# Block-sparse attention and a gated feed-forward on one core: attention output turned by DMA transposes, attention packed into the first half of the output stage, loads tied to the gate/value stages

## The chip, the core and the metric

The kernel runs on one core of a Trainium2 chip. The core has five engines with their own instruction queues: TensorE (PE, matmuls and weight loads), VectorE (DVE), ScalarE (ACT), GpSimd (POOL) and SyncE (SP, which here only issues DMAs). Each executes its queue in order; they wait for each other through semaphores. DMAs issued by SyncE and by GpSimd share the core's 16 DMA engines. The metric is the device time of one execution in microseconds, the median of several runs; smaller is better.

## The reference

Inputs q, k and v have 4 batches, 8 heads, 768 positions and 64 features. Each query attends to keys less than 16 positions away and, beside them, to 24 block summaries (one per 32 keys). The result, as a matrix x of 3072 tokens by 512 features, goes through a gated feed-forward layer with a gated residual.

```python
k_sum = k.reshape(B, H, nb, block, D).max(axis=3)     # block 32, nb 24
v_sum = v.reshape(B, H, nb, block, D).mean(axis=3)
scores_l = scale * q @ k^T, masked to |i - j| < 16
scores_s = scale * q @ k_sum^T + log(32)
a = softmax(concat(scores_l, scores_s))
x = a @ concat(v, v_sum)                              # -> [3072, 512]
g = x @ w_gate;  val = x @ w_val                      # 512 -> 1536
ffn_out = (gelu(g) * val) @ w_out                     # 1536 -> 512
out = x + sigmoid(x @ w_res) * ffn_out
```

## The kernel before

**Units and stages.** The tokens are worked in 8 units (u = 0 to 7) of 384 tokens, two for each batch b: half = 0 and half = 1. The loop over units is at the end of the kernel. For each unit there is a gate/value stage and an output stage. The gate/value stage runs 12 steps over fo (fo_step): four matmuls for g and four for vv (one for each quarter ko of the 512 features of x, L307), Gelu on ScalarE (L312), and the product gvT on VectorE (L313). g and vv live in PSUM tiles with the tag mm, of which there are four (ps_mm). The output stage of unit u (mid_out for u = 1 to 6, first_out for 0, last_out for 7) works, for each of three groups (sub) of 128 tokens, a residual gate (res_step: r, then tanh), 12 matmuls over gvT and w_out (ffn_step: f, L339), and a closing step on VectorE (end_step: th, o) that ends in an output DMA on SyncE.

**Attention inside the output stage.** While unit u's output stage runs, the attention of unit u+1 is worked between its matmuls. For each of four head pairs hp: s_step (12 small matmuls of kW against qT, L267, into the one PSUM buffer of ps_s; exp on ScalarE to P, L271; mask on VectorE, L274), and later av_step (12 small matmuls of P against vext, L285; reciprocal L289 and product L291 on VectorE give xn). Then xt_step turns the 128 features of a pair with three TensorE transposes (xp, L296), and VectorE copies them (L298) to xT, whose quarters ko the next gate/value stage reads as the moving operand. s_step, av_step and xt_step are written into mid_out by hand, and their place in the code is their place in each engine's queue.

**Keys, queries and values of the next batch.** For batch 0 and 1, k and q are turned on TensorE (k_step, q_step). For batches 2 and 3 they are loaded by GpSimd DMAs, cast to bf16, into k_nat (12 DMAs) and q_nat (6 DMAs) (load_nat), followed by 12 v loads into vext (v_loads). turn_all then issues two DMA transposes on SyncE: k_nat to kW (L124) and q_nat to qT (L126). It stands after step fo = 6 of the gate/value stage of units 2 and 4; the loads are first in the code of those units, and nothing but free buffers holds GpSimd back from issuing them. In the gate/value stages of units 3 and 5, v_rims copies the neighbouring rows of v by DMAs on SyncE, vsum_grp computes block means of v (12 matmuls, a VectorE cast to vpart, four small SyncE DMAs to vsum), vsum_bc spreads them with four GpSimd copies (L257), and k_blocks, after steps fo = 4 to 7, computes the block maxima of k for one head pair (L199 reduce, L203 copy, both VectorE). k_rims (GpSimd, L207 and L208) copies neighbouring key columns after the transpose of k.

The lines that the steps of the prediction touch:

```python
xn = st["xn"].rearrange("p s (h d) -> p s h d", d=D)[:, :, 2 * hp:2 * hp + 2, :]   # [128, NSUB, DM]
nc.tensor.transpose(xp[:, sub * 128:(sub + 1) * 128],
                    st["xn"][:, sub, ko * 128:(ko + 1) * 128], ident[:])
copy(st["xT"][:, ko, :], xp[:])
```

Of the kernel before, what the change touches and what calls it, by code (L numbers as in the profile page):

```python
# [9 lines left out]
BF16 = mybir.dt.bfloat16  # L10
# [5 lines left out]
def kernel(  # L16
# [11 lines left out]
    nc = tc.nc  # L28
# [41 lines left out]
    bgrp = const.tile([QT, 3, 32], BF16, name="bgrp")  # L70
    warm = const.tile([128, 512], BF16, name="warm")
    gate1 = const.tile([1, 1], F32, name="gate1")
    kW = [const.tile([128, NT, NP, 128], BF16, name=f"kW{i}") for i in range(2)]
    qT = [const.tile([128, NQ, NP, 128], BF16, name=f"qT{i}") for i in range(2)]
    k_nat = const.tile([QT, NT, DM], BF16, name="k_nat")
# [9 lines left out]
    def load_qk(src, b, parts, name):  # L85
        t = qk.tile([PP, H, PJ, D], BF16, tag=name, name=name)
        hs = H // parts
        for i in range(parts):
            nc.gpsimd.dma_start(
                out=t[:, i * hs:(i + 1) * hs].rearrange("p h j d -> p h (j d)"),  # L90
                in_=src[b, i * hs:(i + 1) * hs].rearrange("h (p j) d -> p h (j d)", j=PJ),
            )
        return t
# [18 lines left out]

    k_sb, q_sb = {}, {}

    def load_nat(b):
        for t in range(NT):
            nc.gpsimd.dma_start(out=k_nat[:, t].rearrange("p (h d) -> p h d", d=D),  # L117
                                in_=k[b, :, t * QT:(t + 1) * QT, :].rearrange("h p d -> p h d"))
        for c in range(NQ):
            nc.gpsimd.dma_start(out=q_nat[:, c].rearrange("p (h d) -> p h d", d=D),  # L120
                                in_=q[b, :, c * 128:(c + 1) * 128, :].rearrange("h p d -> p h d"))

    def turn_all(b):
        nc.sync.dma_start_transpose(out=kW[b % 2].rearrange("d t g k -> d (t g) k")[:, :, 0:QT],  # L124
                                    in_=k_nat.rearrange("p t f -> p (t f)"))
        nc.sync.dma_start_transpose(out=qT[b % 2].rearrange("d c g k -> d (c g) k"),  # L126
                                    in_=q_nat.rearrange("p c f -> p (c f)"))

    with tc.manual_schedule():
# [147 lines left out]
        def av_step(u, hp, st, pool=ps_o, tag="ao"):  # L277
            b, half = u // 2, u % 2
            P = st["P", hp]
            ao = pool.tile([128, NSUB, 2, D + 1], F32, tag=tag, name="ao")  # L280
            for sub in range(NSUB):
                for hh in range(2):
                    for e in range(2):
                        t = 2 * sub + e
                        nc.tensor.matmul(ao[64 * e:64 * e + 64, sub, hh, :], P[:, hh, t, :],  # L285
                                         vext[b % 2][:, half * HT + t, 2 * hp + hh, 0:D + 1],
                                         start=True, stop=True, skip_group_check=True)
            rz = work.tile([128, NSUB, 2, 1], F32, tag="rz", name="rz")
            nc.vector.reciprocal(rz[:], ao[:, :, :, D:D + 1])  # L289
            xn = st["xn"].rearrange("p s (h d) -> p s h d", d=D)[:, :, 2 * hp:2 * hp + 2, :]  # L290
            nc.vector.tensor_mul(xn, ao[:, :, :, 0:D], rz.to_broadcast([128, NSUB, 2, D]))  # L291

        def xt_step(u, ko, st, pool, tag, copy=nc.vector.tensor_copy):
            xp = pool.tile([128, TU], BF16, tag=tag, name="xp")
            for sub in range(NSUB):
                nc.tensor.transpose(xp[:, sub * 128:(sub + 1) * 128],  # L296
                                    st["xn"][:, sub, ko * 128:(ko + 1) * 128], ident[:])
            copy(st["xT"][:, ko, :], xp[:])  # L298

        def new_unit():  # L300
            return {"xn": upool.tile([128, NSUB, DM], BF16, tag="xn", name="xn"),
                    "xT": upool.tile([128, KO, TU], BF16, tag="xT", name="xT")}


# [13 lines left out]
        def fo_step(st, gvT, fo):  # L318
# [3 lines left out]
            gv_mm(vv, w_val, st, fo, range(KO))  # L322
            gv_end(gvT, fo, g, vv)

        def res_step(st, sub):
            ss = slice(sub * 128, (sub + 1) * 128)
            r = mm_tile("r")
            for ko in range(KO):
                nc.tensor.matmul(r[:], st["xT"][:, ko, ss], w_res[:, ko, :],  # L329
                                 start=(ko == 0), stop=(ko == KO - 1))  # L330
            st["th", sub] = work.tile([128, DM], F32, tag="th", name="th")
            nc.scalar.activation(st["th", sub][:], r[:], AF.Tanh, scale=0.5)  # L332

        def ffn_step(st, gvT, sub, lo, hi):
            ss = slice(sub * 128, (sub + 1) * 128)
            if lo == 0:
                st["f", sub] = mm_tile("f")
            for fo in range(lo, hi):
                nc.tensor.matmul(st["f", sub][:], gvT[:, fo, ss], w_out[:, fo, :],  # L339
                                 start=(fo == 0), stop=(fo == FO - 1), skip_group_check=True)  # L340

        def end_part(u, st, sub, f, cs):
            th = st["th", sub]
            n = cs.stop - cs.start
            nc.vector.scalar_tensor_tensor(th[:, cs], th[:, cs], 1.0, f[:, 0:n], ALU.add, ALU.mult)  # L345
            o = work.tile([128, n], F32, tag="o", name="o")
            nc.vector.scalar_tensor_tensor(o[:], th[:, cs], 0.5, st["xn"][:, sub, cs], ALU.mult, ALU.add)  # L347
            row = u * TU + sub * 128
            nc.sync.dma_start(out=out[row:row + 128, cs], in_=o[:])

# [121 lines left out]

        def mid_out(u, st, gvT, nst):
            n = u + 1
            s_step(n, 0, nst)
            res_step(st, 0)
            ffn_step(st, gvT, 0, 0, FO)
            av_step(n, 0, nst)
            s_step(n, 1, nst)
            end_step(u, st, 0)  # L480
            res_step(st, 1)
            ffn_step(st, gvT, 1, 0, 4)
            av_step(n, 1, nst)
            s_step(n, 2, nst)
            ffn_step(st, gvT, 1, 4, FO)
            av_step(n, 2, nst)
            s_step(n, 3, nst)
            xt_step(n, 0, nst, ps_t, "t")
            end_step(u, st, 1)
            res_step(st, 2)  # L490
            ffn_step(st, gvT, 2, 0, 4)
            av_step(n, 3, nst)
            xt_step(n, 1, nst, ps_t, "t")
            ffn_step(st, gvT, 2, 4, FO)
            xt_step(n, 2, nst, ps_t, "t")
            xt_step(n, 3, nst, ps_mm, "mm")
            end_step(u, st, 2)

        def last_out(u, st, gvT):
# [4 lines left out]
                end_step(u, st, sub)  # L504
            last_step(u, st, gvT, NSUB - 1)

        for u in range(NU):
            b, half = u // 2, u % 2
            nb = b + 1
            if half == 0 and nb < B:  # L510
                if nb == 1:
                    k_sb[nb] = load_qk(k, nb, 1, "k_sb")
                    v_loads(nb)
                    for i in range(2):
                        q_sb[2 * nb + i] = load_q(nb, i)
                else:
                    load_nat(nb)
                    v_loads(nb)
            if u:
                gvT = upool.tile([128, FO, TU], BF16, tag="gvT", name="gvT")  # L520
            for fo in range(0 if u else 2, FO):
                fo_step(st, gvT, fo)
                if u == 0 and fo >= 8:
                    q_step(0, 1, fo - 8, ps_t, "t")
                if u == 2 and fo < NP:
                    q_step(1, 1, fo, ps_t, "t")
                if half == 0 and 1 < nb < B and fo == 6:
                    turn_all(nb)
                    k_rims(nb, slice(0, NP), nc.gpsimd)
                if half == 1 and nb < B:  # L530
                    if fo == 0:
                        v_rims(nb, 0, NT)
                    if fo == (4 if nb == 1 else 0):
                        vsum_grp(nb, ps_t, "t")
                        for i in range(4):
                            vsum_bc(nb, 3 * i, 3 * i + 3, nc.gpsimd)
                    if nb == 1:
                        if fo < NP:
                            k_step(nb, fo, ps_t, "t")
                        elif 7 <= fo < 7 + NP:  # L540
                            q_step(nb, 0, fo - 7, ps_t, "t")
                    elif 4 <= fo < 4 + NP:
                        k_blocks(nb, fo - 4)
            if u == NU - 1:
                last_out(u, st, gvT)
            else:
                nst = new_unit()
                (mid_out if u else first_out)(u, st, gvT, nst)
                st = nst
# [30 lines left out]
```

The softmax here doesn't subtract the row's maximum and nothing guards it: scores larger than these inputs give would overflow.

## Time and profile before

| what | value |
|---|---|
| median of 4 runs | 277.73 us (277.55 to 277.99) |
| the profiled execution | 278.43 us, of which the span of the instructions is 276.7 us |
| granted TensorE clock, mean | 0.997 |
| busy: TensorE, VectorE, ScalarE, GpSimd | 265.1, 162.0, 128.5, 101.0 us |
| transposes of x on TensorE (xp) | 96, of which 72 in the six stages of mid_out |
| q0 (GpSimd's DMAs) | 14.69 MB |
| q1 (SyncE's DMAs) | 10.96 MB |

The profile is of one execution. Spans, starts and durations are microseconds from the span's start unless marked ns. A group of instructions is named by its line, engine and the tiles it writes and reads. The chain that ended last is followed back from the last instruction, at each step to what released it. Matmuls are pipelined, and the chain counts them from end to end, so that its lengths add up. A DMA's row on SPq or POOL is the time that the issuing engine spent on it; its landing comes later.

### The profile page before, as it was taken

Reading aid. Unit: us, or ns where it says so; the run is one execution under the profiler, and the core shown is the slowest. Engines: PE = TensorE matmul, PEld = TensorE weight load, DVE = VectorE, ACT = ScalarE, POOL = GpSimd, SP = SyncE. Lnnn points to the kernel's source line nnn. Section 1 sums busy time; section 2 is a strip of 40 time slices with the busy share of each in tenths; the row PEclk is TensorE's granted clock in tenths of the full one; section 3 lists DMA queues with packets and bytes.
Section 4 is the critical chain, followed back from the end, with each engine's and each line's share of the span. In section 5 each row is a group of like instructions: output and inputs, shape, how many; then the busy total and the mean of one; then the engine's idle time right before and its main releaser. Section 6 shows DMA issues by size and latency. Waiting matters only on the chain.

```text
span 276.7 us, 5879 instructions
## 1 busy us (share of the span) xinstructions
PE 265.1 (96%) x2377; PEld 142.8 (52%) x2377; DVE 162.0 (59%) x365; ACT 128.5 (46%) x204; POOL 101.0 (36%) x134
## 2 busy tenths in 40 slices
PE   7889989999999999999899999999899999999994
PEld 2445644555545555446444565446444565555543
DVE  5856423598338533685947743685947743684424
ACT  1776347375565446343255336343256336343320
POOL 8795572340699942000799832000800000000000
PEclk9999999999999999999999999999999999999998
DMA  6999999999089999114099998104001100111003
GB/s 89 167 130 200 196 204 206 157 157 168 5 53 140 188 154 153 39 39 94 2 69 130 194 168 130 40 38 94 2 0 40 76 2 0 40 39 40 0 0 114
DMA packets 91274, 26.00 MB, mean 94 GB/s; under 512 B 75176, under 2 KB 88304, under 8 KB 91248
## 3 DMA queue, kind: packets, MB, share of 16 engines
q0 software_dynamic: 63664, 14.69, 57.4%
q1 hardware_dynamic: 27584, 10.96, 19.0%
q8 instruction: 18, 0.29, 0.4%
q14 instruction: 8, 0.07, 0.1%
HBM read 29.36 MB, written 6.29 MB: 129 GB/s over the span
## 4 chain that ended last, share of the span: by engine, by line
PE 76%; DMA 11%; DVE 5%; POOL 4%; issue 2%; ACT 1%; POOLq 0%; DVEq 0%
PE f L339 21%; PE g L307 19%; PE vv L307 18%; PE r L329 7%; DMA w_out<-in_moe_w_out_dram 5%; DMA w_gate<-in_moe_w_gate_dram 4%; PE ao L285 3%; PE s L267 3%; DMA q_sb<-in_q_dram 3%; PE xp L296 2%; DVE ks L199 2%; DVE gvT L313 2%; POOL vext L104 1%; PE f L360 1%; PE tp L224 1%
## 5 line engine op out<-in xcount | busy, mean ns | idle before, releaser
L313 DVE TENSOR_TENSOR gvT<-ge,vv 128x384 bf16<-128x384 f32 x96 | 52.6, 552 | 58.7 <-PE vv L307 56.6
L312 ACT ACTIVATE ge<-g 128x384 f32<-128x384 f32 x96 | 47.0, 490 | 82.8 <-DVE gvT L313 42.9
L307 PE MATMUL g<-xT,w_gate 128*128 128x384 bf16 x384 | 80.1, 326 | 1.8 <-DVE gvT L313 1.4
L307 PE MATMUL vv<-xT,w_val 128*128 128x384 bf16 x384 | 78.4, 326 | 1.0 <-DVE gvT L313 1.0
L339 PE MATMUL f<-w_out,gvT 128*128 128x512 bf16 x276 | 65.5, 379 | 0.1
L307 PEld LDWEIGHTS <-w_val 128*128 128x128 bf16 x384 | 37.4, 98 | 27.1 <-issue 2.7
L307 PEld LDWEIGHTS <-w_gate 128*128 128x128 bf16 x384 | 35.7, 98 | 26.8 <-issue 5.0
L271 ACT ACTIVATE P<-s,bias_t 128x768 bf16<-128x768 f32 x32 | 28.8, 901 | 31.8 <-PE s L267 31.6
L257 POOL COPY vext<-vsum 32x1536 bf16<-32x1536 bf16 x14 | 20.0, 1465 | 62.6 <-DMA vsum<-vpart 62.6
L339 PEld LDWEIGHTS <-gvT 128*128 128x128 bf16 x276 | 26.0, 98 | 29.7 <-DMA w_out<-in_moe_w_out_dram 0.6
L104 POOL DMA_DIRECT2D vext<-in_v_dram x48 | 33.0, 731 | 14.5 <-DMA w_out<-in_moe_w_out_dram 5.6
L274 DVE TENSOR_TENSOR P<-P,maskt 128x768 bf16<-128x768 bf16 x32 | 17.7, 556 | 20.6 <-ACT P L271 18.9
L329 PE MATMUL r<-w_res,xT 128*128 128x512 bf16 x96 | 24.3, 381 | 0.0
L345 DVE SCALAR_TENSOR_TENSOR th<-th,f 128x512 f32<-128x512 f32 (+1 forms) x25 | 16.5, 658 | 6.1 <-PE f L339 5.8
L291 DVE TENSOR_TENSOR xn<-ao,rz 128x384 bf16<-128x384 f32 x32 | 17.8, 557 | 1.1
L347 DVE SCALAR_TENSOR_TENSOR o<-th,xn 128x512 f32<-128x512 f32 (+1 forms) x25 | 16.8, 670 | 0.9
L117 POOL DMA_DIRECT2D k_nat<-in_k_dram x24 | 16.3, 749 | 0.0
L199 DVE TENSOR_REDUCE ks<-kW 128x24 bf16<-128x768 bf16 x16 | 15.1, 943 | 1.6 <-ACT kW L214 1.5
L332 ACT ACTIVATE th<-r 128x512 f32<-128x512 f32 x24 | 14.2, 594 | 3.4 <-PE r L329 2.9
L285 PEld LDWEIGHTS <-P 128*64 128x64 bf16 x384 | 8.7, 110 | 13.6 <-DVE P L274 6.4
L289 DVE RECIPROCAL rz<-ao 128x6 f32<-128x6 f32 x32 | 6.1, 192 | 16.2 <-PE ao L285 16.1
L285 PE MATMUL ao<-vext,P 128*64 128x65 bf16 x384 | 12.2, 199 | 0.7 <-DVE vext L238 0.7
(69 smaller groups left out, 189.4 us busy)
## 6 DMA issues: line engine op xcount, KB each, us to landing
out_dram<-o SPq DMA_DIRECT2D x23, 256.0 KB
vext<-in_v_dram POOLq DMA_DIRECT2D x48, 64.0 KB, 6.2
q_sb<-in_q_dram POOLq DMA_DIRECT2D x4, 384.0 KB, 8.7
w_gate<-in_moe_w_gate_dram POOLq DMA_DIRECT2D x6, 256.0 KB, 9.9
w_val<-in_moe_w_val_dram POOLq DMA_DIRECT2D x6, 256.0 KB, 10.7
w_out<-in_moe_w_out_dram POOLq DMA_DIRECT2D x3, 512.0 KB, 14.1
k_nat<-in_k_dram POOLq DMA_DIRECT2D x24, 64.0 KB, 3.1
q_nat<-in_q_dram POOLq DMA_DIRECT2D x12, 128.0 KB, 5.8
```

Source lines behind the costliest of these rows:

```text
L104: nc.gpsimd.dma_start(out=vext[b % 2][0:QT, t, :, 0:D], in_=v[b, :, t * QT:(t + 1) * QT, :].rearrange("h p d -> p h d"))
L199: nc.vector.tensor_reduce(out=ks.rearrange("d (t n) -> d t n", n=2), in_=kw[:, :, 0:QT].rearrange("d t (n w) -> d t n w", w=BLK), axis=myb ...
L257: eng.tensor_copy(vext[b % 2][96:128, lo:hi, :, 0:D], src)
L271: nc.scalar.activation(P.rearrange("p a t q -> p a (t q)"), s[:, :, 0:TU], AF.Exp, scale=scale, bias=bias_t[:])
L274: nc.vector.tensor_mul(Pf, Pf, maskt.unsqueeze(1).to_broadcast([128, 2 * HT, QT]))
L285: nc.tensor.matmul(ao[64 * e:64 * e + 64, sub, hh, :], P[:, hh, t, :], vext[b % 2][:, half * HT + t, 2 * hp + hh, 0:D + 1], start=True, st ...
L291: nc.vector.tensor_mul(xn, ao[:, :, :, 0:D], rz.to_broadcast([128, NSUB, 2, D]))
L307: nc.tensor.matmul(ps[:, 0:TU], w[:, ko, fo * 128:(fo + 1) * 128], st["xT"][:, ko, :], start=(ko == 0), stop=(ko == KO - 1), skip_group_ch ...
L312: nc.scalar.activation(ge[:], g[:, 0:TU], AF.Gelu)
L313: nc.vector.tensor_mul(gvT[:, fo, :], ge[:], vv[:, 0:TU])
L329: nc.tensor.matmul(r[:], st["xT"][:, ko, ss], w_res[:, ko, :], start=(ko == 0), stop=(ko == KO - 1))
L339: nc.tensor.matmul(st["f", sub][:], gvT[:, fo, ss], w_out[:, fo, :], start=(fo == 0), stop=(fo == FO - 1), skip_group_check=True)
```

## The change

- xn gets the layout [128, KO, NSUB, 128], so that the features of one head pair lie together. The last VectorE operation of end_part reads it in that shape.
- For units 2 to 7 (the attention that mid_out works) xt_step is replaced by xt_dma: one DMA transpose per head pair, issued by SyncE right after that pair's av_step. Unit 1 (first_out) keeps xt_step.
- In mid_out all four s_steps and av_steps stand among the matmuls of the first token group; av_step alternates between the PSUM pools ps_o and ps_t. res_step and ffn_step of groups 1 and 2 follow, and end_step of group 0 comes after the last av_step.
- fo_first (units 2 to 7) works quarters 0 to 2 of both g and vv before quarter 3 of both. fo_last_two (units 1 to 7) works g of the last two steps before vv of both.
- load_nat and turn_all are split. pool_after, a one-element GpSimd copy that reads the product gvT of step 0, stands ahead of the k and v loads (units 2 and 4, after step 0) and of the q loads (units 3 and 5, after step 0). turn_k stays after step 6 of units 2 and 4; turn_q goes to step 1 of units 3 and 5, after vsum_grp and vsum_bc, which move there from step 0.
- v_rims is split: the lower half at step 0 of odd units, the upper half at step 1 of the next even unit. k_blocks goes from steps 4 to 7 to steps 8 to 11; since steps 10 and 11 are worked together at step 10, two of them come after the stage's last product.

```diff
+        def xt_dma(ko, st):
+            nc.sync.dma_start_transpose(out=st["xT"][:, ko].rearrange("d (s k) -> d s k", k=128),
+                                        in_=st["xn"][:, ko].rearrange("p s d -> p (s d)"))
...
-            return {"xn": upool.tile([128, NSUB, DM], BF16, tag="xn", name="xn"),
+            return {"xn": upool.tile([128, KO, NSUB, 128], BF16, tag="xn", name="xn"),
...
+        def fo_first(st, gvT):
+            g, vv = mm_tile("g"), mm_tile("vv")
+            for kos in (range(KO - 1), (KO - 1,)):
+                gv_mm(g, w_gate, st, 0, kos)
+                gv_mm(vv, w_val, st, 0, kos)
+            gv_end(gvT, 0, g, vv)
+
+        def fo_last_two(st, gvT):
+            g = [mm_tile("g"), mm_tile("g")]
+            for i in range(2):
+                gv_mm(g[i], w_gate, st, FO - 2 + i, range(KO))
+            for i in range(2):
+                vv = mm_tile("vv")
+                gv_mm(vv, w_val, st, FO - 2 + i, range(KO))
+                gv_end(gvT, FO - 2 + i, g[i], vv)
...
         def mid_out(u, st, gvT, nst):
             n = u + 1
+            other = dict(pool=ps_t, tag="t")
             s_step(n, 0, nst)
             res_step(st, 0)
-            ffn_step(st, gvT, 0, 0, FO)
+            ffn_step(st, gvT, 0, 0, 2)
+            s_step(n, 1, nst)
+            ffn_step(st, gvT, 0, 2, 5)
             av_step(n, 0, nst)
-            s_step(n, 1, nst)
+            xt_dma(0, nst)
+            ffn_step(st, gvT, 0, 5, 6)
+            s_step(n, 2, nst)
+            ffn_step(st, gvT, 0, 6, 8)
+            av_step(n, 1, nst, **other)
+            xt_dma(1, nst)
+            ffn_step(st, gvT, 0, 8, 9)
+            s_step(n, 3, nst)
+            ffn_step(st, gvT, 0, 9, FO)
+            av_step(n, 2, nst)
+            xt_dma(2, nst)
+            res_step(st, 1)
+            av_step(n, 3, nst, **other)
+            xt_dma(3, nst)
             end_step(u, st, 0)
-            res_step(st, 1)
-            ffn_step(st, gvT, 1, 0, 4)
-            av_step(n, 1, nst)
-            s_step(n, 2, nst)
-            ffn_step(st, gvT, 1, 4, FO)
-            av_step(n, 2, nst)
-            s_step(n, 3, nst)
-            xt_step(n, 0, nst, ps_t, "t")
+            ffn_step(st, gvT, 1, 0, FO)
+            res_step(st, 2)
             end_step(u, st, 1)
-            res_step(st, 2)
-            ffn_step(st, gvT, 2, 0, 4)
-            av_step(n, 3, nst)
-            xt_step(n, 1, nst, ps_t, "t")
-            ffn_step(st, gvT, 2, 4, FO)
-            xt_step(n, 2, nst, ps_t, "t")
-            xt_step(n, 3, nst, ps_mm, "mm")
+            ffn_step(st, gvT, 2, 0, FO)
             end_step(u, st, 2)
...
+        def pool_after(x):
+            nc.gpsimd.tensor_copy(gate2[:], x)
...
+                if half == 0 and 1 < nb < B and fo == 0:
+                    pool_after(gvT[0:1, 0, 0:1])
+                    load_k_nat(nb)
+                    v_loads(nb)
+                if half == 0 and b and fo == 1:
+                    v_rims(b, HT, NT)
                 if half == 0 and 1 < nb < B and fo == 6:
-                    turn_all(nb)
+                    turn_k(nb)
                     k_rims(nb, slice(0, NP), nc.gpsimd)
                 if half == 1 and nb < B:
                     if fo == 0:
-                        v_rims(nb, 0, NT)
-                    if fo == (4 if nb == 1 else 0):
+                        v_rims(nb, 0, HT)
+                        if nb > 1:
+                            pool_after(gvT[0:1, 0, 0:1])
+                            load_q_nat(nb)
+                    if fo == (4 if nb == 1 else 1):
                         vsum_grp(nb, ps_t, "t")
                         for i in range(4):
                             vsum_bc(nb, 3 * i, 3 * i + 3, nc.gpsimd)
+                        if nb > 1:
+                            turn_q(nb)
...
-                    elif 4 <= fo < 4 + NP:
-                        k_blocks(nb, fo - 4)
+                    elif 8 <= fo < 8 + NP:
+                        k_blocks(nb, fo - 8)
```

## The prediction

> **What bounds the kernel now.** I read the page's busy table first, then the chain that ended last, stage by stage.
>
> ```profile
> PE 265.1 (96%) x2377; PEld 142.8 (52%) x2377; DVE 162.0 (59%) x365; ACT 128.5 (46%) x204; POOL 101.0 (36%) x134
> PE 76%; DMA 11%; DVE 5%; POOL 4%; issue 2%; ACT 1%; POOLq 0%; DVEq 0%
> ```
>
> From about 56 us on TensorE is the chain. So time goes if a matmul leaves TensorE's queue or a gap in it closes, and comes if TensorE waits for something new. The chain of one output stage (unit 4) and the start of the next gate/value stage (columns: start, length, what):
>
> ```profile
> 179.38 0.31 PE ao L285 x12
> 179.69 0.28 PE s L267 x12
> 179.97 0.27 PE xp L296 x3
> 180.25 0.86 PE r L329 x4
> ...
> 182.28 0.27 PE xp L296 x3
> 182.56 1.73 PE f L339 x8
> 184.28 0.34 PE xp L296 x6
> 184.62 0.87 PE g L307 x4
> 185.49 0.65 PE vv L307 x4
> ```
>
> The transposes (xp) lie on the path, and the first g group takes 0.87 us where later ones take 0.65, because its last transposed quarter comes late: 0.22 us. The stage takes 13.92 us (170.70 to 184.62). A plain gate/value stage is 15.82 (216.89 to 232.71): 24 groups of 0.65 plus that 0.22. Stages of units 3 and 5 hold the value-sum matmuls too (0.76), so should take 16.58, but take 18.64 (122.31 to 140.95) and 18.35 (184.62 to 202.97). VectorE and GpSimd there (start, length):
>
> ```profile
> 133.04 1.52 DVE L203 COPY kW<-ks 128x288 bf16<-128x288 bf16 x1
> ...
> 138.74 0.23 DVE L203 COPY kW<-ks 128x288 bf16<-128x288 bf16 x1
> ```
>
> ```profile
> 133.01 5.71 POOL L257 COPY vext<-vsum 32x1536 bf16<-32x1536 bf16 x4 [23.99 <-DMA vsum<-vpart]
> ```
>
> The same VectorE copy takes 0.23 us alone and 1.5 beside the GpSimd broadcast. The gvT products queue behind it, PSUM buffers come free late, and TensorE loses 2.06 + 1.77 = 3.8 us. Last, the DMA transposes that exist already, on SyncE's queue, and the q loads ahead of them:
>
> ```profile
> 157.41 5.88 SPq L124 DMA_TRANSPOSE kW<-k_nat  x1
> 163.60 5.36 SPq L126 DMA_TRANSPOSE qT<-q_nat  x1
> ```
>
> ```profile
> 146.68 5.39 POOL L120 DMA_DIRECT2D q_nat<-in_q_dram  x6
> ...
> 168.55 0.77 POOL L207 COPY kW<-kW 128x704 bf16<-128x704 bf16 x1 [7.14 <-DMA kW<-k_nat]
> ```
>
> kW lands at 168.55, 5.3 us after its issue ended, with v loads in flight. The DMA engines fall quiet at about 170.4, so qT lands some 1.4 us after its issue ends (168.96). In the earlier pair the issues took 6.97 and 7.68.
>
> [...] the issues take 7 us beside more load traffic, 5.4 beside less. [...] The trace moved 284 and 290 GB/s at 168 to 170 us, so 5.36 us may be contention rather than the transpose's own cost.
>
> **The change, part by part.** T is the start of a gate/value stage, S of an output stage.
>
> *Transposes off TensorE, six output stages.* By matmul starts the 12 transposes fill 0.18 + 0.18 + 0.33 = 0.69 us. The late 0.22 goes as well, since fo_first uses quarter 3 last, a microsecond into the stage. The new order changes between small attention tiles and full matmuls more often. Such a change costs 0.1 (r 0.97 after s against 0.86, f 1.83 against 1.73); I count eight places (each s before r or f, each av before r or f) against five, so +0.3. Net -0.61, times 6: **-3.7 us**. VectorE's 24 copies (0.35 each) leave too, worth nothing by themselves as VectorE is 8.7 of 14 us busy there.
>
> *The packed attention.* av 0 is queued S+2.7 after s, r, two f, s, three f (0.28+0.97+0.43+0.28+0.75). Its P needs exp and mask: in the trace P was ready 2.75 us after s began, 1.28 of it table load. fo_last_two computes both last g groups 1.3 us before the stage's end, so the last Gelu and the table load lie under vv; P is then ready by about S+2.1. The single s buffer is freed by each exp about 1.0 us after its s; the next s comes 1.3, 1.35 and 1.15 later. That cover is 0.15 to 0.35 us. Price without it: perhaps 0.5 a stage. I take 0.
>
> *The DMA transposes of x.* One is an eighth of qT's, so 5.36/8 = 0.67 us of issue by proportion. xn of pair 0 is ready at S+4.2, of pair 3 at S+8.1; the last is issued by S+8.9 and lands about 2 us later, S+11. It is needed at S+13.5 plus a microsecond. I take 0; a fixed cost per transpose that the two large ones can't show is bounded below by 0. Up to about 2.3 us each the four still fit (4.2+4x2.3+1.5 = 14.9); beyond that TensorE waits in all six stages. Behind them on SyncE are only the output stores, for which nobody waits with three o buffers.
>
> *k and v loads gated, units 2 and 4.* The gate opens at T+2.2 (gv product of fo 0). Twelve k loads (8.2 to 9 us) end at T+11.3, land 3.1 later; turn_k waits on SyncE until T+14.3 and issues to T+20.2. Queued behind it: the x transposes, whose first input is ready at S+4.2 = T+20.0. kW lands by T+25.5, twelve v loads (0.7 each, to T+19.7) competing; the x quarters follow by about T+27. They are needed at T+29.2. Hidden, 2 us to spare; beyond that it costs one for one, twice. The gate keeps k loads out of the output stage but not the last v loads, which run some 4 us into it. v_rims, k_rims and the next vsum read these data a stage later.
>
> *q gated, units 3 and 5: a new wait on the path.* Gate at T+2.2; six q loads end issue at T+7.6. In the trace q loads landed 1.3 us apart (4.2 us after the first issue, 6.5 after the last, 4.3 later). First landing about T+5.5, last T+12 beside other loads, nearer T+10.5 alone: T+11.5. turn_q then takes 5.36 + 1.4: qT lands at T+18.3. The first s of the output stage reads it and is queued at T+16.4 (24x0.65+0.76). **Wait 1.9 us.** Ends: 786 KB at 287 GB/s plus 1.4, landing T+15.6, no wait; the slow issue of 7.68 and loads at T+12.5, landing T+21.6, wait 5.2. Behind that s stands all of TensorE.
>
> *k_blocks moved to fo 8 to 11.* The old 3.8 us disappear: **-3.8**. VectorE now has, from the product of fo 8 (T+13.1), two blocks of 1.18 (0.94+0.24), products 9 to 11 (0.55 each), the other two blocks, ending T+19.5; only then the mask of pair 0, 0.56. av 0 stood at T+19.1: 1.0 us. GpSimd's broadcast moves with vsum: cast to T+4.8, four small DMAs (3.0), landed T+8.6, 5.7 of copies to T+14.3, so mostly clear of the blocks; if two copies still meet it, +2.5. This wait overlaps that for qT; the longer counts. I take 2.0 for both stages: **+4.0**.
>
> *Sum.* -3.7 - 3.8 + 4.0 = -3.5. The profiled execution has a span of 276.7 in 278.43, 1.7 lying outside; the median of the runs is 277.73, 0.7 under it. I apply -3.5 to the median: **274.2 us**.
>
> **Rivals.**
> *qT binds (ends slower).* Place: the first s of the output stages of units 3 and 5. The gains are 7.5 us, so the wait decides at 3.75 each: qT landing after T+20.2. For it: the issue of 7.68 and loads landing 6.5 us late give T+21.6, wait 5.2, 277.73 - 7.5 + 10.4 = 280.6. Against: v and k loads, which slowed that issue, are gated elsewhere.
> *qT is early.* The transpose alone runs at 287 GB/s: only the VectorE chain's 1.0 remains, 277.73 - 7.5 + 2.0 = 272.2. For it: the burst at 168 to 170 us. Against: that was a queue already filled.
> *Packed attention leaves gaps.* 0.5 us in six stages: -3.5 + 3.0, 277.2. For it: slack of only 0.15 at the fourth s. Against: VectorE and ACT have room.
> *Small transposes are dear.* At 2.5 us each the last lands at S+4.2+10+1.5 = 15.7, 1.2 late, six times: -3.5 + 7.2, 281.4. For it: no small one was traced. Against: twice as many, smaller blocks in kW cost no more than qT's.
>
> **How the numbers follow.** Forecast 0.49 (all faster, 272.4 to 276.5); qT early 0.15 (faster); gaps 0.11 (0.07 faster, 0.04 same); qT binds 0.18 (0.16 slower, 0.02 same); dear transposes 0.07 (slower). Faster 0.71, same 0.06, slower 0.23; 0.2% is what a measurement of this kernel can tell from no change. Range 272.4 to 278.6: it leaves out the lower half of the early case (0.07) and the upper parts of the two slow ones (0.13). Faster cases alone: 272 to 276.5.
>
> **What would show it.** xp gone from six stages and the first g groups at 0.65; output stages of units 1, 2, 4 and 6 at about 13.5 us; units 3 and 5's gate/value stages near 16.4, followed by a gap of about 2 us, its releaser qT or VectorE's P. SyncE's x transposes near 0.7 us each. I am wrong if that gap exceeds 3.75, if g waits for xT, or if s and ao wait in the ordinary stages.

## The result

The changed kernel takes 280.01 us (median of 34 runs, 277.27 to 283.88) against 277.97 for the kernel before beside it: a ratio of 1.0054, with a 95% interval of 1.0039 to 1.0069. (The ratio leaves out runs more than 1.5% above the fastest of their kernel, here six of the changed one's 34; the two medians alone give 1.0073.) It is slower by half a per cent, where 274.2 us and a gain had been forecast. The profiled execution took 281.13 us, with a span of 279.3 (before: 278.43 and 276.7), so the span to explain is +2.6 us.

The page of the changed kernel (busy time; granted TensorE clock in 40 slices; the two DMA queues with packets, MB and share of 16 engines' time; the chain that ended last):

```profile
PE 264.5 (95%) x2305; PEld 139.6 (50%) x2305; DVE 155.5 (56%) x341; ACT 128.7 (46%) x204; POOL 102.3 (37%) x138
PEclk9999999999999999999979999999979999999999
q0 software_dynamic: 63664, 14.69, 59.4%
q1 hardware_dynamic: 37664, 13.32, 25.0%
PE 72%; DMA 18%; POOL 5%; ACT 2%; DVE 1%; issue 1%; POOLq 0%; SPq 0%
```

The queues of the kernel before:

```profile
q0 software_dynamic: 63664, 14.69, 57.4%
q1 hardware_dynamic: 27584, 10.96, 19.0%
```

The 72 transposes are gone from TensorE (2377 matmuls before, 2305 now), but its busy time fell by only 0.6 us, and the chain has moved from TensorE (76% to 72%) to DMAs (11% to 18%). Two slices of the clock row show a 7. And q0 carries the same packets and bytes as before for 59.4% of 279.3 = 165.9 us, against 57.4% of 276.7 = 158.8 us. Nothing in the change asks more of that queue. This was the first sign of the cause found below.

TensorE's waits, and then its timeline around the first of them (columns: start, us, instruction, idle time before it and its releaser):

```profile
PE s L272 <- DMA qT<-q_nat: 4.5, 2, 2.4
PE s L272 <- ACT P L276: 1.6, 2, 1.1
```

```profile
142.14 0.35 PE L272 MATMUL s<-qT,kW 64*128 64x64 bf16 x12 [2.36 <-DMA qT<-q_nat]
142.42 1.04 PE L354 MATMUL r<-w_res,xT 128*128 128x512 bf16 x4
144.54 1.46 PE L364 MATMUL f<-w_out,gvT 128*128 128x512 bf16 x3
```

The wait for qT is where the forecast put it, 2.36 us in unit 3 and 2.13 in unit 5 (forecast 1.9). What the forecast doesn't have is what follows. The windows of that place (after the engines' busy shares: granted clock, DMA share, GB/s):

```profile
143.00:144.00 1.00, 1.00 (x5) 0.20 (x2) 0.99 (x2) 0.93 (x2) 0.00 (x0) 0.74 0.00 0
145.00:146.00 1.00, 1.00 (x5) 0.16 (x5) 0.41 (x1) 0.55 (x1) 0.00 (x0) 0.50 0.00 0
```

TensorE stays busy but at half speed: three f matmuls take 1.46 us, where the same group takes 0.82 at full clock (in a run shown later). The trace's record of the clock has exactly two such stretches inside the work, 3.41 us each: one begins 1.3 us after the first wait for qT (at 143.47), the other as the second ends (at 204.91). Idle times of 2.36 and 2.13 us were enough for it here; what decides it is worked out after the experiments.

The two other steps, in the places where the prediction showed them before. The end of unit 4's output stage on the chain:

```profile
182.96 0.86 PE r L354 x4
183.82 2.59 PE f L364 x12
186.41 0.49 PE g L316 x3
```

Here the stage runs from 172.84 to 186.41, so 13.57 us against 13.92. VectorE's block copies and GpSimd's broadcast in unit 3's gate/value stage:

```profile
137.44 0.94 DVE L208 COPY kW<-ks 128x288 bf16<-128x288 bf16 x1
139.73 1.46 DVE L208 COPY kW<-ks 128x288 bf16<-128x288 bf16 x1
```

```profile
135.41 5.69 POOL L262 COPY vext<-vsum 32x1536 bf16<-32x1536 bf16 x4 [3.99 <-DMA vsum<-vpart]
```

They still meet: the forecast had the broadcast finished by T+14.3, and it runs from T+12.1 to T+17.8. But the blocks now stand near the last products, and the gate/value stage loses nothing to them: it takes 16.47 us (123.31 to 139.78, where the wait for qT begins) against 18.64. SyncE's transposes:

```profile
136.60 3.66 SPq L131 DMA_TRANSPOSE qT<-q_nat  x1
```

```profile
L306 SPq DMA_TRANSPOSE xT<-xn x24: 1177/1202/2225, 83.3 to 244.4; - x24
DMA to landing us min/median/max: 2.3/3.0/8.1
```

(Duration in ns: least, median, most; first and last start.) qT's transpose issues faster than forecast (3.66 against 5.36 us), and lands 1.8 us after its issue. A transpose of x issues in 1.2 us, not 0.67, and stays hidden: no g waits for xT.

**Where the 2.6 us come from.** The table gives the lengths between first g groups on TensorE's timeline: up to unit 1's, then from each unit's to the next, and from unit 7's to the span's end. The first three rows are what is needed here; the others belong to the experiments.

| | to unit 1 | unit 1 | 2 | 3 | 4 | 5 | 6 | 7 | span |
|---|---|---|---|---|---|---|---|---|---|
| before | 56.34 | 34.48 | 31.33 | 32.56 | 29.75 | 32.27 | 29.74 | 30.2 | 276.7 |
| forecast, change | 0 | -0.61 | -0.61 | -0.67 | -0.61 | -0.38 | -0.61 | 0 | -3.5 |
| after | 57.19 | 35.20 | 30.76 | 33.93 | 29.17 | 33.74 | 29.17 | 30.1 | 279.3 |
| after, again (e9) | 58.43 | 35.19 | 30.76 | 33.85 | 29.17 | 32.32 | 29.18 | 30.1 | 279.0 |
| shift of 64 bytes (e10) | 56.12 | 35.19 | 30.76 | 31.80 | 29.17 | 31.58 | 29.17 | 30.1 | 273.9 |
| no shift, halves (e12) | 55.85 | 35.19 | 30.76 | 31.49 | 29.17 | 31.09 | 29.17 | 30.1 | 272.8 |
| combined (e7) | 55.85 | 34.13 | 30.76 | 30.04 | 29.18 | 31.30 | 29.18 | 30.1 | 270.5 |
| combined, shift (e11) | 56.96 | 34.13 | 30.76 | 30.04 | 29.17 | 30.04 | 29.17 | 30.0 | 270.3 |

(Forecast for unit 3: -0.61 - 2.06 + 2.0; for unit 5: -0.61 - 1.77 + 2.0.) The ordinary units 2, 4 and 6 gain 0.57 to 0.58 each, as forecast. Four places miss: before unit 1 +0.85, unit 1 +0.72 where -0.61 was forecast, unit 3 +1.37, unit 5 +1.47.

### The profile page after: what moved, and what is told of

It reads as the page before. It is cut to its first block, busy times and chain, and to the rows that moved or that the text cites. A ratio compares the mean times of both kernels' runs of the same rounds, so it can differ in the third digit from the quotient of the medians.

```text
span 279.3 us, 5801 instructions
## 1 busy us (share of the span) xinstructions
PE 264.5 (95%) x2305; PEld 139.6 (50%) x2305; DVE 155.5 (56%) x341; ACT 128.7 (46%) x204; POOL 102.3 (37%) x138
## 3 DMA queue, kind: packets, MB, share of 16 engines
q0 software_dynamic: 63664, 14.69, 59.4%
## 4 chain that ended last, share of the span: by engine, by line
PE 72%; DMA 18%; POOL 5%; ACT 2%; DVE 1%; issue 1%; POOLq 0%; SPq 0%
PE f L364 22%; PE g L316 17%; PE vv L316 16%; PE r L354 7%; DMA w_out<-in_moe_w_out_dram 5%; DMA qT<-q_nat 4%; DMA w_gate<-in_moe_w_gate_dram 4%; PE ao L290 3%; PE s L272 3%; DMA q_sb<-in_q_dram 3%; DMA q_nat<-in_q_dram 2%; POOL q_nat L123 2%; POOL vext L105 1%; PE f L388 1%; PE tp L229 1%
## 5 line engine op out<-in xcount | busy, mean ns | idle before, releaser
L316 PE MATMUL g<-xT,w_gate 128*128 128x384 bf16 x384 | 78.6, 327 | 0.1
L364 PE MATMUL f<-w_out,gvT 128*128 128x512 bf16 x276 | 70.4, 387 | 0.6 <-DMA w_out<-in_moe_w_out_dram 0.6
L364 PEld LDWEIGHTS <-gvT 128*128 128x128 bf16 x276 | 25.0, 98 | 27.8 <-DMA w_out<-in_moe_w_out_dram 1.1
L279 DVE TENSOR_TENSOR P<-P,maskt 128x768 bf16<-128x768 bf16 x32 | 17.8, 558 | 22.3 <-ACT P L276 20.7
L354 PE MATMUL r<-w_res,xT 128*128 128x512 bf16 x96 | 25.1, 391 | 0.4 <-DMA w_res<-in_moe_w_res_dram 0.4
L296 DVE TENSOR_TENSOR xn<-ao,rz 128x384 bf16<-128x384 f32 x32 | 17.8, 557 | 1.1
L272 PE MATMUL s<-qT,kW 64*128 64x64 bf16 x384 | 11.6, 195 | 6.1 <-DMA qT<-q_nat 4.5
L540 POOL COPY gate<-gvT 1x1 bf16<-1x1 bf16 x4 | 0.7, 180 | 41.8 <-DVE gvT L322 41.8
```

The costliest lines, as they stand in the source:

```text
L272: nc.tensor.matmul(s[:, hh, t * QT:(t + 1) * QT], kw[ps, tt, hp, :], qt[ps, tt // 2, hp, (tt % 2) * QT:(tt % 2 + 1) * QT], start=True, sto ...
L279: nc.vector.tensor_mul(Pf, Pf, maskt.unsqueeze(1).to_broadcast([128, 2 * HT, QT]))
L316: nc.tensor.matmul(ps[:, 0:TU], w[:, ko, fo * 128:(fo + 1) * 128], st["xT"][:, ko, :], start=(ko == 0), stop=(ko == KO - 1), skip_group_ch ...
```

## The experiments

The first theory (A) was the simplest: the wait for qT and the slow clock after it are the loss; take the wait away and the forecast's gain appears. The rival (B) was that q's transfer would only push the wait elsewhere.

**e1: q earlier.** The six q loads go out behind the v loads of units 2 and 4, under the same gate; turn_q stays.

```diff
                     load_k_nat(nb)
                     v_loads(nb)
+                    load_q_nat(nb)
...
-                        if nb > 1:
-                            pool_after(gvT[0:1, 0, 0:1])
-                            load_q_nat(nb)
```

> The changed kernel with one thing undone: the q loads follow the v loads in units 2 and 4 again, behind the same gate as k and v, so that only turn_q stays in units 3 and 5. Theory A (the loss is TensorE's wait for qT, 2.36 and 2.13 us, and the lowered TensorE clock after each wait, some 3.4 us at about 0.5, so 1.7 us lost each): both disappear; VectorE's chain of k_blocks may leave 1 to 1.5 us of waiting in each of the two output stages. 280.0 - 2 x (3.9 - 1.5) = 275 us, granted clock 0.997 or more. Rival B (the packed order and the small transposes cost what was gained, and the qT wait only covers VectorE's chain): 279 us or more.

Measured: 281.04 us (280.21 to 284.55), ratio 1.0093 (1.0076 to 1.0109). The wait for qT is gone, but the list of TensorE's waits now has this first:

```profile
PE g L316 <- DMA xT<-xn: 4.1, 6, 0.9
```

The transposes of x, which land at most 8.1 us after their issue in the changed kernel, land up to 10.0 us after it here, and the only edit is that the q loads now follow the v loads in units 2 and 4. Theory A's number failed; whether the loads alone do this, or only together with the slower DMAs found below, wasn't tried.

**e2: keep the clock up.** Nine matmuls on a constant tile, whose result nobody uses, stand ahead of the first s of the output stages of units 3 and 5. q comes no sooner; most of the idle time goes (1.19 us of it stay in unit 3 of the profile).

```diff
             other = dict(pool=ps_t, tag="t")
+            if u in (3, 5):
+                wf = ps_o.tile([128, 512], F32, tag="ao", name="wf")
+                for _ in range(9):
+                    nc.tensor.matmul(wf[:], warm[:, 0:128], warm[:], start=True, stop=True)
             s_step(n, 0, nst)
```

> The changed kernel with the wait for qT kept, but nine matmuls on a constant tile (9 x 0.215 = 1.9 us, result unused) put into TensorE's queue ahead of the first s of the output stages of units 3 and 5, where it only waits. Theory A1 (the clock falls because TensorE idles in the wait): the wait ends at the same time, the clock stays at 0.997 or more, and the time is 280.0 - 2 x 1.7 = 276.6 to 277.4 us with little spread. Rival A2 (the clock falls for another reason): clock near 0.988 and 280 us as before. If the queued matmuls themselves delay the stage, 281 us.

Measured: 278.70 us (276.86 to 281.21), 1.0022 (1.0005 to 1.0038), so 0.9 us under the changed kernel by the two ratios (1.3 by the medians) although work was added. A mean clock of at least 0.997 (one stretch of 3.41 us at half speed takes 0.006 off it) was seen in 15 of 22 runs, against 7 of 34 of the changed kernel. So idling does bring the clock down, and that is part of the loss. But it is not all: what is left is still above before.

**e3: unit 1.** On top of e1, unit 1's q_steps stand one step earlier.

```diff
-                        elif 7 <= fo < 7 + NP:
-                            q_step(nb, 0, fo - 7, ps_t, "t")
+                        elif 6 <= fo < 6 + NP:
+                            q_step(nb, 0, fo - 6, ps_t, "t")
```

It goes after unit 1's +0.72. ScalarE there, in the changed kernel:

```profile
77.85 0.48 ACT L231 COPY qT<-tp 128x384 bf16<-128x384 bf16 x1 [1.10 <-PE tp L229]
78.35 1.28 ACT L276 ACT_TABLE_LOAD   x1
79.64 0.90 ACT L276 ACTIVATE P<-s,bias_t 128x768 bf16<-128x768 f32 x1
```

The last q_step comes after fo_last_two, which now works steps 10 and 11 together, so its copy follows the last Gelu instead of preceding it. The table load of 1.28 us, which fo_last_two was to hide under vv, waits for that copy, and the second s waits 1.10 us for the exp.

> As e1, and in unit 1 the four q_steps one step earlier (after steps 6 to 9 instead of 7 to 10), so that no ScalarE copy of q stands between the last Gelu and the table load for exp. Theory A (that copy moved the table load to 0.6 us after s began, and the second s waited 1.1 us for the single s buffer): 1.1 us less than e1, about 274 us. Rival (the wait in unit 1 has another cause): as e1.

Measured: 280.26 us (278.97 to 282.10), 1.0083 (1.0050 to 1.0116). Unit 1 takes 34.13 us, 1.07 less than in the changed kernel: that part is settled. The time as a whole hides it, since this profile has a wait at the very start, 3.7 us for the v rims, with 6.8 us at half clock:

```profile
PE ao L290 <- DMA vext<-vext: 3.7, 1, 3.7
```

Nothing that e3 changed has run by then.

**e4: the key blocks earlier.** On top of e3, k_blocks after steps 1 to 4 in place of 8 to 11.

```diff
-                    elif 8 <= fo < 8 + NP:
-                        k_blocks(nb, fo - 8)
+                    elif 1 <= fo < 1 + NP:
+                        k_blocks(nb, fo - 1)
```

> As e3, and k_blocks after steps 1 to 4 in units 3 and 5 instead of 8 to 11, ahead of the GpSimd broadcast. If VectorE's chain of k_blocks (four times 1.18 us, two copies slowed to 1.5 us beside the broadcast) delays the first mask in e1 and e3: 2 to 3 us less than e3, about 271.5 us, and the output stages of units 3 and 5 as long as those of 2 and 4 (13.5 us). Rival (the chain is hidden): as e3.

Measured: 278.60 us (276.33 to 281.57), 1.0013 (0.9997 to 1.0029): better than e3 by 1.7 us, but far from the 271.5 expected, again with 2.0 us of waiting for the v rims at the start and 3.2 us for xT.

**The new suspect.** Both unexplained things, the early wait and the longer busy time of q0, are about DMAs that the change doesn't touch. What it does touch is their addresses. pool_after writes to a new tile, gate2, of one element, which stands ahead of kW and moves every later tile by 32 bytes in each partition: kW begins at byte 18,944 before, and at 18,976, no multiple of 64, after.

**e5: no shift.** The element goes into a second column of gate1, which has room for it. No later tile moves; the instructions are the same.

```diff
-    gate1 = const.tile([1, 1], F32, name="gate1")
-    gate2 = const.tile([1, 1], BF16, name="gate2")
+    gate1 = const.tile([1, 2], F32, name="gate1")
...
-        nc.scalar.activation(gate1[:], bias_t[0:1, :], AF.Gelu)
+        nc.scalar.activation(gate1[:, 0:1], bias_t[0:1, :], AF.Gelu)
...
-            nc.gpsimd.tensor_copy(gate2[:], x)
+            nc.gpsimd.tensor_copy(gate1[:, 1:2], x)
```

> The changed kernel, with the one-element target of pool_after put into the second element of the tile gate1 instead of a tile of its own, so that all later tiles keep the addresses that they have in the kernel before (kW0 at 18944 instead of 18976). Theory S: the 32 bytes by which the new tile shifts every later tile slow the DMAs (the profile before: 57.4% of 276.7 = 158.8 us on the queue of GpSimd's DMAs; after: 59.4% of 279.3 = 165.9 us, for the same packets and bytes): back to about 159 us, loads land earlier, the wait for qT shrinks to about 1.5 us, fewer clock falls, 277.5 to 278.5 us with less spread. Rival: addresses don't matter, 280 us.

Measured: 275.50 us (274.94 to 279.08, 22 runs), 0.9907 (0.9889 to 0.9925). The same instructions at other addresses are faster than before by 0.9%. (The profiled execution, 279.08 us, is the slowest of the 22; e10 below gives the better profile.) The gain is larger than expected.

**e6: the kernel before, with the shift.** A tile of one element in gate2's place, written once.

```diff
+    pad = const.tile([1, 1], BF16, name="pad")
+    tc.nc.vector.memset(pad[:], 0.0)
```

> The kernel before with a tile of one element (32 bytes with its padding, and one memset of it) put where the changed kernel has its new one, so that later tiles are shifted by 32 bytes; nothing else. Theory S: GpSimd's queue goes from 159 to about 166 us, and the time rises by 0.5 to 1 us (the weight loads of the first 45 us and their stages are DMA-bound), with more spread. Rival: 278.0 us as the kernel before.

Measured: 278.76 us (277.74 to 280.70), 1.0010 (0.9985 to 1.0036). In the kernel before, the shift costs nothing that can be told from no change: q0 is busy for 161.5 us against 158.8, not for the 166 expected, and the stretch before unit 1 is 0.7 us longer, but no long wait of TensorE hangs on those DMAs. It isn't quite without trace: in 10 of the 14 runs the mean clock is under 0.997, in the kernel before beside them in 2 of 37.

**e7: all repairs.** e5, with q turned in two halves (so that the first can start when three of the six loads have landed; in unit 3 it begins at about T+10), unit 1's q_steps as in e3, k_blocks as in e4.

```diff
-                            turn_q(nb)
+                            turn_q(nb, 0, NQ // 2)
+                            turn_q(nb, NQ // 2, NQ)
```

> The changed kernel without the address shift, q loaded as in it, but turned in two transposes (the three chunks of the next unit first), q_step of unit 1 one step earlier, and k_blocks after steps 1 to 4. The half that the next output stage needs lands at about T+14.5, before s at T+16.4. If the qT wait, VectorE's chain, unit 1's table load and the shift are the whole loss: 277.97 - 3.7 - 3.8 = 270.5 to 272 us, clock 0.997 or more. If the packed order or the small transposes are themselves at fault: 276 us or more.

Measured: 271.41 us (270.65 to 272.50), 0.9742 (0.9705 to 0.9780). It beats both kernels. TensorE waits for no qT, and no stretch of half clock lies inside the work.

**e8: no shift, and the nine matmuls of e2.**

> As e5 with the nine matmuls of e2 in the wait. Theory A1 and S together: the clock stays at 0.997 or more and the runs lie close together, 276 to 277 us; less than e5 by what the clock costs (up to 1.7 us for each fall). If S is wrong, as e2 (278.7).

Measured: 276.44 us (276.29 to 277.13, 8 runs), 0.9931 (0.9905 to 0.9956). In this timeline the added work ends where the wait would have:

```profile
138.49 2.11 PE L506 MATMUL wf<-warm 128*128 128x512 bf16 x9
140.53 0.35 PE L271 MATMUL s<-qT,kW 64*128 64x64 bf16 x12
142.50 0.82 PE L363 MATMUL f<-w_out,gvT 128*128 128x512 bf16 x3
```

All 8 runs keep a clock of 0.997 or more. But without the shift 19 of e5's 22 do so anyway, so 2.1 us of filling costs more than it saves. The shift costs this pair 278.70 against 276.44 (ratios 1.0022 and 0.9931).

**e9 to e12** ran together on one chip, to rule out that chip and session made the difference, and to separate alignment from a mere move. e9 is the changed kernel once more, e10 has gate2 64 bytes wide, e11 is e7 with gate2 as its own tile, e12 is e5 with the halved turn of q alone.

```diff
-    gate2 = const.tile([1, 1], BF16, name="gate2")
+    gate2 = const.tile([1, 32], BF16, name="gate2")
...
-            nc.gpsimd.tensor_copy(gate2[:], x)
+            nc.gpsimd.tensor_copy(gate2[:, 0:1], x)
```

> The changed kernel as it is, on the chip of the next three. Theory A (the 32 bytes that gate2 moves every later tile by cost about 4 us): 279.5 to 280.5, q0 busy for 165 us, and at least 3 us above the versions without the shift. Theory B (the gap between 280.0 and e5's 275.5 was the chip and the day): 275.5 to 276.5 here.

> The changed kernel with gate2 64 bytes wide (one element is written as before), so that the later tiles stand 64 bytes beyond their places in the kernel before and start on multiples of 64 bytes again. Alignment theory (a start that is no multiple of 64 bytes slows the DMAs that write and read the tiles): 275 to 276, q0 busy for 160 us. Rival (any move of the tiles, or the tile itself, costs it): 279.5 to 280.5, q0 busy for 165 us.

> e7 with gate2 as a tile of its own again, so with the 32-byte shift. If slower DMAs cost only where a wait for qT is left to lengthen: 271.4 to 272.5, no wait for qT over 0.3 us. If the shift costs in every version of the change as it does between after and e5: 275 to 276.

> e5 with one edit of e7 alone: q is turned by two transposes of three chunks each in place of one of six. If the two waits for qT (4.1 us in e5's profile) and the clock that falls after them are what is left above the forecast's case without them: 271.5 to 273, no wait for qT over 0.3 us. If e7's gain came from the key scores ahead of their place and from the query projection of unit 1: 275 to 276, with the waits moved to another transpose.

| | kW at byte | us (median, range) | ratio to before (95%) |
|---|---|---|---|
| e9, changed kernel again | 18,976 | 281.00 (279.45 to 281.93) | 1.0101 (1.0067 to 1.0135) |
| e10, shift of 64 bytes | 19,008 | 275.91 (275.02 to 278.91) | 0.9936 (0.9911 to 0.9960) |
| e11, combined, with shift | 18,976 | 272.38 (271.37 to 272.99) | 0.9789 (0.9757 to 0.9821) |
| e12, no shift, q in halves | 18,944 | 274.62 (274.50 to 274.84) | 0.9874 (0.9848 to 0.9900) |

e9 and e10 have the same instructions; e10 moves the tiles twice as far and is 5.1 us faster. So it is neither the added tile nor a move as such nor the chip, but a move by 32 bytes, which 32 more undo. q0's time agrees: 59.0% of 279.0 = 164.6 us in e9 and 58.3% of 273.9 = 159.7 in e10, as expected.

Which tiles matter is open. kW, qT, k_nat, q_nat, vext, vsum, vpart, the weights, k_sb and q_sb start on multiples of 64 bytes before, in e5 and in e10, and 32 bytes past one in the changed kernel and e9. For ge, th, o, P, xn, xT and gvT it is the other way round, because the three buffers of rz, which are allocated between the two groups, take 32 bytes each. The x transposes, between tiles of the second group, issue in the same time in e9 and e10 (median 1.21 us) and land after 3.1 and 2.8 us. Loads into tiles of the first group land later in e9: those of k after 4.1 against 3.5 us, those of q after 5.3 against 4.8. That points to the first group, but no run moves one group alone.

e9's queue and its first long wait:

```profile
q1 hardware_dynamic: 37664, 13.32, 24.9%
```

```profile
22.82 0.35 PE L290 MATMUL ao<-vext,P 128*64 128x65 bf16 x11 [2.45 <-DMA vext<-vext]
```

and e10's queue, its waits for qT, and the first s of unit 3's output stage:

```profile
q1 hardware_dynamic: 37664, 13.32, 23.3%
```

```profile
PE s L272 <- DMA qT<-q_nat: 2.5, 2, 1.3
```

```profile
140.36 0.35 PE L272 MATMUL s<-qT,kW 64*128 64x64 bf16 x12 [1.23 <-DMA qT<-q_nat]
```

q1's packets, SyncE's transposes and rims among them, take 24.9% of 279.0 = 69.5 us in e9 and 23.3% of 273.9 = 63.8 us in e10 (69.8 in the changed kernel, 63.5 in e5). The single packet is not slower. The median of q1's 256-byte packets, the size of the transposes' packets, is 18 ns in all four of these runs, and those of the x transposes take about 20 ns on average in e9 and e10 alike when nothing else moves. What grows is the tail: the 256-byte packets of more than twice the median add up to 15.2 us of engine time in the changed kernel and 14.8 in e9, but to 9.8 in e5 and 9.7 in e10, and the 128-byte packets of q0 likewise to 8.4 and 7.0 against 2.5 and 2.7. Nor is the transpose of q itself slower: its issues take 3.87 and 3.99 us in e9, 3.64 and 4.25 in e10. It begins 0.5 us later in its stage in e9, in both units, behind the later q loads.

The effect on the time is larger than that on the packets because of where it falls, as the rows of the stage table show. Before unit 1: 2.3 us between e9 and e10. In all eight profiles with the shift unit 1's stage begins at 56.9 us or later (up to 60.2), in all six without it at 56.8 or earlier (the nearest two are 0.15 us apart); a long wait for the v rims at the start, as in e9, stands in three of the eight (e3, e4 and e9) and in none of the six. Unit 3: 2.05 us, of it 0.99 in a longer wait (2.22 against 1.23) and the rest in the clock, which falls after the longer one alone. Unit 5: 0.74 us, with a wait of 1.95 against 1.27, and no fall in either. Together 5.1, the whole of the difference.

e10's tiles stand 64 bytes off their places in the kernel before (kW at 74 x 256 + 64 in place of 74 x 256), and that costs nothing that shows: 275.91 us, against 275.50 for e5, where they stand in their old places (ratios to before of 0.9936 and 0.9907, intervals that overlap). So in these runs it is the place against 64 bytes that counts. Why it is wasn't tried.

e11 says when the shift matters. Once qT is early enough, it costs 272.38 against 271.41, intervals that overlap, with 1.1 us of it before unit 1 in the profiles (56.96 against 55.85).

e12 was to tell how much of e7 is due to q alone. It takes 0.9 us off e5, less than expected, because with qT there in time the next in line shows:

```profile
PE ao L289 <- DVE P L278: 2.2, 2, 1.3
```

That is the mask behind VectorE's k_blocks, 1.26 us in unit 3 and 0.98 in unit 5, where the forecast had 1.0 each, overlapped by the wait for qT. e7 removes it by placing k_blocks after steps 1 to 4 (before: 4 to 7): unit 3 falls from 31.49 to 30.04. The moved q_steps take 1.06 us off unit 1. In unit 5 this e7 profile loses 1.1 us to g waiting for gvT (31.30), which e11's doesn't (30.04), so that the two profiles differ by 2.3 us where the medians differ by 3.2.

**When the clock falls.** The length of a wait doesn't decide it alone: 2.13 us in the changed kernel's unit 5 halved the clock, 1.95 us in e9's did not. In all 14 profiles every change of the granted clock lies a whole number of steps of 3.413 us after the start of that trace's clock record (40, 41, 58, 59 and 80 steps in the changed kernel), and the record starts anywhere from 4.2 to 7.3 us after the span's start. Cut into these steps, the 14 profiles have 1098 at full clock. After 23 of them the clock halves, nine times inside the work and 14 times where it ends: in each of the 23, TensorE has no matmul for 53% of the step or more. In each of the other 1075 it has none for at most 49%, and the clock stays. Some of these steps:

| run | step, us | TensorE busy in it, us | next step |
|---|---|---|---|
| changed kernel, wait of 2.36 us | 140.06 to 143.47 | 1.33 | half clock |
| changed kernel, wait of 2.13 us | 201.50 to 204.91 | 1.38 | half clock |
| e1, waits for xT of 0.94, 0.24 and 0.92 us | 184.75 to 188.16 | 1.31 | half clock |
| e9, first part of the wait of 1.95 us | 201.39 to 204.80 | 2.64 | full clock |
| e9, the rest of that wait | 204.80 to 208.21 | 2.23 | full clock |
| e10, wait of 1.23 us | 138.30 to 141.72 | 2.17 | full clock |

So in these traces the clock falls after a step of which more than half was idle. A wait under 1.7 us doesn't fill half a step by itself; a longer one may or may not, by how it lies across the steps, and their place differs from one execution to the next. (When the clock comes back is not covered by this: in e4 a step at half clock with 25% idle was followed by another at half.)

## Why the prediction was wrong

Its sum was -3.5 us, the profile's is +2.6. Of the 6.1 us between, 2.0 are unit 3's, 1.9 unit 5's, 1.3 unit 1's and 0.85 lie before unit 1.

- *Transposes off TensorE, -0.61 a stage:* right, 0.57 to 0.58 in units 2, 4 and 6. In unit 1 it failed, by 1.3 us: "fo_last_two computes both last g groups 1.3 us before the stage's end, so the last Gelu and the table load lie under vv" left out the q_step copy queued behind that Gelu (shown by e3, e7 and e11, 34.13 us there).
- *The packed attention at 0:* right in units 2, 4 and 6, where neither s nor ao waits.
- *DMA transposes of x at 0.67 us:* mis-sized by proportion; 1.2 us each. The forecast let them go up to 2.3 unseen, and they stayed unseen.
- *k and v loads hidden, 2 us to spare:* right; no wait for kW, and none for xT in the changed kernel. e1 shows that six more loads use up the spare time.
- *q gated, wait 1.9 us:* the place and very nearly the size were right: 2.36 and 2.13 us, and in e10, without the 32-byte offset, 1.23 and 1.27. There qT is ready at about T+18.2 in unit 3, where the forecast had T+18.3, but in part by luck: turn_q begins at T+12.6, not T+11.5, and its issue takes 3.64 us, not 5.36; s is queued at about T+17.0, not T+16.4. The step that failed is the price of the wait, taken one for one. A wait of more than 1.7 us can leave TensorE idle for over half of a 3.413 us step, and in these 14 profiles the clock then halved for the next; the forecast's own 1.9 us was already long enough for it. It did so after the waits of 2.1 to 2.4 us (the changed kernel, unit 3 of e5 and e9), and not after those of 1.2 to 2.0 (e10, unit 5 of e5 and e9). Unit 3 shows the price: 1.13 us more of wait from e10 to the changed kernel cost 2.13; unit 5: 0.86 more cost 2.16. So a fall costs 1.0 to 1.3 us beside the wait.
- *k_blocks moved, -3.8 and +1.0 behind the wait for qT:* right. The wait for the mask is 1.26 and 0.98 once it shows (e12).
- *What the forecast didn't list at all:* the address of every tile behind gate2. The tile is in the diff, and its price wasn't asked for. With kW and the tiles behind it back on multiples of 64 bytes the change gives 275.5 (e5) to 275.9 us (e10), a gain of 0.6 to 0.9%, inside the forecast's range and 1.3 to 1.7 above its time; unit 1's 1.3 is the largest term of that. The 32 bytes turned this gain into a loss: 1.1 to 2.3 us before unit 1 (the changed kernel and e9 against e10), and waits for qT long enough to leave over half of a step idle. A mean clock of 0.997 or more is seen in 7 of the 40 runs with the shift (the first and e9), and in 31 of 36 without (e5 and e10).

Of the rivals, *qT binds* named the right place, and by its own condition (3.75 us each) it did not come true; that its 280.6 us lies near the measured 280.0 is chance. Of the signs of being wrong, neither a gap over 3.75 us nor a g that waits for xT came; s waited in unit 1 alone. *Packed attention leaves gaps* and *small transposes are dear* did not occur.

## What to carry to other kernels

A new small tile moves everything allocated behind it: give it a place in an existing tile or at the end, or pad it to 64 bytes, so that the tiles behind it that DMAs write and read keep their places against multiples of 64 bytes (here 275.50 us in an existing tile and 275.91 padded, against 280.01 and 281.00). When a change leaves a wait on TensorE of more than half of the 3.413 us seen here, price it with the chance that the clock halves after it (here 1.0 to 1.3 us beside the wait), and prefer to shorten the wait (here by turning q in halves, 274.62 us) over filling it (276.44 us). A sum over stages should be checked in the stages with extra passengers, like unit 1's q_step: the order that was to hide a table load of 1.28 us exposed it there, for 1.10 us of waiting.

## What was not expected of the hardware

- Moving kW and all tiles behind it by 32 bytes slows this kernel's DMAs: 69.5 against 63.8 us of q1's packet time for the same packets, 281.00 against 275.91 us for the same instructions. Moving them by 64 bytes costs nothing that shows (275.91 us against 275.50 without a move). The median 256-byte packet of q1 takes the same 18 ns; those of more than twice that add up to 14.8 us in place of 9.7.
- TensorE's clock halved for 3.41 us whenever TensorE had been idle for 53% or more of a step at full clock, 3.413 us long and on a fixed grid, and never when it had been idle for 49% or less (1098 steps at full clock in 14 profiles). So one wait of 2.1 us did it, three of 0.94, 0.24 and 0.92 us within 2.8 us did it, and one of 1.95 us that lay across two steps did not.
- A DMA transpose of 128 x 384 bf16 out of and into SBUF issues in 1.2 us, while one of eight times the size took 3.25 to 4.25 us in the changed kernel and e5: far from proportional.
